# Layer 2's attention scores in the 64-row tile shape of the products, two heads per weight

## The chip, the cores and the metric

One Trainium2 chip, one of its cores. The metric is the device time of one launch in microseconds: the median of repeated runs. A profiled execution gives the trace; its span runs from the first to the last instruction on the core.

## The reference

Two rounds of attention and feed-forward over a sequence of 2048 tokens of width 448, all in bfloat16:

```python
x = x + A(layernorm(x)); x = x + B(layernorm(x))     # layers 0 and 1
x = x + A(layernorm(x)); x = x + B(layernorm(x))     # layers 2 and 3, same weights

def A(x):                       # H = 16 heads of 28
    q, k, v = heads(x @ wqkv)
    idx = pos[:, None] - 2 * arange(8)[None, :]      # 8 keys, every second token back
    logits = einsum("hsd,hswd->hsw", q, k[:, idx]) * 28**-0.5     # where idx >= 0
    return concat(einsum("hsw,hswd->hsd", softmax(logits), v[:, idx])) @ wo

def B(x):                       # width 1792, no nonlinearity
    return ((x @ w_gate) * (x @ w_up)) @ w_down
```

## The kernel before

The tokens are held with even and odd ones apart (two halves of 1024 columns), so that every second token back becomes the last eight columns of the same half. The sequence is cut into chunks of 256 or 512 tokens for each layer, and `SEQ` names the order of the chunk jobs: attention chunks (`A00` is layer 0, chunk 0) are mixed with feed-forward chunks, so that one layer's small matmuls lie among another's large products.

Nothing is scheduled at run time. Python code records operations (`sc.add`) with their engine, dependences and PSUM banks, and the tables `ORD` (for each engine, the order of operations by number) and `BANK` (the banks each takes) say in full how they stand. Waits are derived from the dependences. In `ORD["pe"]` an entry such as `253+349@24.30.42` means that a run of small matmuls (253) is cut at those places and strips of a large product (349, its host) are put in the gaps; a letter after `!` only orders waits.

The work of one attention chunk:

- `ln_chunk` normalises blocks of 128 tokens (VectorE, two small ScalarE steps), and `xn_sb` is transposed into `xnT`, by TensorE in the head of the kernel (`Tps`, line 638), else by DMAs on SyncE's queue.
- `qk_chunk` makes queries and keys (`WQK`): `twin` runs each product as two row halves of the array at once, 64 rows by 128 columns each; a unit's second half waits for its first half on TensorE itself (`crossed`). The result is copied to `qk` by ScalarE or VectorE (line 732). A head of 28 takes 32 rows, so four heads stand in 128 rows.
- `v_group` makes values, one product for two query blocks, copied to `v_sb` in one instruction (line 824). The last four heads' values go another way, through DRAM (`PW`, `VT`, on SyncE).
- `attn_front` makes scores of a group of two query blocks (120 queries each, 128 keys each, in two halves `c` of 64 keys): 64 matmuls of 28 rows by 64 columns (line 842), for each of 4 head columns, 2 blocks, 2 key halves and 4 heads; then two exponentials on ScalarE (line 849) and two mask multiplications on VectorE (line 859, `MK`). The first group has one block and 32 matmuls.
- `attn_back` multiplies with the values (line 879, 64 rows by 32 columns), `norm` divides, and `y_blocks` makes the output product with `wo_g`.

`b_chunk` makes gate and up (`Gps`, `Ups`), copies one (`G`, line 970), multiplies (`H`, line 973) and makes the down product (`WD`). Plain products are recorded in line 362, strips of hosts in lines 365 and 369. Warm-up matmuls (line 535) fill the head; weights are copied into `WQK` in line 544, mostly by GpSimd, which also makes the masks (lines 515, 519).

Of the kernel before, what the change touches and what calls it, by code (L numbers as in the profile page):

```python
# [3 lines left out]
dt = mybir.dt  # L4
ACT = mybir.ActivationFunctionType
ALU = mybir.AluOpType
# [49 lines left out]
FILL = 9  # L56
ORD = {
# [56 lines left out]

# [9 lines left out]
class Sched:  # L124
# [21 lines left out]
    def schedule(self):  # L146
# [29 lines left out]
        for e in self.ENGS:  # L176
            for x in ORD[e].split():
                ids, _, hint = x.partition("!")
                ids, _, cuts = ids.partition("@")
                ids, _, pre = ids.partition("~")  # L180
                burst, *hosts = [self.ops[int(i)] for i in ids.split("+")]
                pre = int(pre or 0)
                if pre:
                    for op in hosts:
                        take(op, e)
                    order[e].append((hosts, [(op, n) for op in hosts for n in range(2 * pre)], hint[:1]))
                    hint = hint[1:]
                    take(burst, e)
                else:
                    for op in (burst, *hosts):  # L190
                        take(op, e)
                seq = [(burst, n) for n in range(len(burst.ins))]
                if hosts:
                    strips = self.strips(x, hosts, pre, len(cuts.split(".")))
                    done = pre + len(strips) // len(hosts)
                    seq, a = [], 0
                    for i, z in enumerate([int(c) for c in cuts.split(".")] + [len(burst.ins)]):
                        seq += [(burst, n) for n in range(a, z)]
# [4 lines left out]
                order[e].append(([burst] if pre else [burst, *hosts], seq, hint))  # L203
# [194 lines left out]
def build(nc, A_x, A_wqkv, A_wo, B_w_gate, B_w_up, B_w_down, out):  # L398
# [35 lines left out]
    ones32 = sb([128, 128], bf, "ones32")  # L434
    MK = sb([128, 3, 72], bf, "MK")
    ident = sb([128, 128], bf, "ident")
# [679 lines left out]
```

## Time and profile before

| | |
|---|---|
| median of 3 runs | 384.57 us (384.23 to 384.86) |
| profiled execution | 384.47 us, span 382.7 us |
| TensorE | busy 377.9 us (99%), 6406 matmuls |
| VectorE | busy 268.9 us (70%) |
| ScalarE | busy 198.7 us (52%) |
| GpSimd | busy 10.4 us (3%) |
| granted TensorE clock | 0.999 of full speed |

Line numbers are those of the kernel before. A matmul's row gives its operand as rows * columns of the weight, then the moving operand. Matmuls overlap in the array, so the time of a stretch is read from the start of its first matmul to the start of the next stretch.

### The profile page before, as it was taken

How to read it: one execution, taken by the hardware profiler on the slowest of the kernel's cores; microseconds unless marked ns; L12 is line 12 of the kernel's file. 1: busy time of each engine (PE TensorE's matmuls, PEld its weight loads, DVE VectorE, ACT ScalarE, POOL GpSimd, SP SyncE). 2: the span in 40 equal slices, each digit the busy share in tenths (PEclk: the TensorE clock that was granted, in tenths of full speed). 3: DMA queues.
4: the chain of work that ended last, by engine and by line, in shares of the span. 5: the costliest groups of instructions: out<-in, count | busy, mean ns of one | idle time of the engine just before them, and what ended most of it. 6: DMA issues, size and time to landing. Idle time of an engine off the chain costs nothing.

```text
span 382.7 us, 14257 instructions
## 1 busy us (share of the span) xinstructions
PE 377.9 (99%) x6406; PEld 209.3 (55%) x6406; DVE 268.9 (70%) x595; ACT 198.7 (52%) x393; POOL 10.4 (3%) x42
## 2 busy tenths in 40 slices
PE   8999999999999999999999999999999999999997
PEld 3556477544555445445466677544555544445764
DVE  5986989788886584885868766666787786355413
ACT  4989986646635672345343664457435542124310
POOL 7210000000000000000000000000000000000000
PEclk9999999999999999999999999999999999999999
DMA  8967422500540026010411425120142005030003
GB/s 271 240 138 204 111 65 44 90 6 15 81 48 16 17 49 77 15 27 15 70 24 29 46 40 83 40 26 4 21 93 45 14 2 108 2 70 6 2 2 120
DMA packets 55103, 22.75 MB, mean 59 GB/s; under 512 B 46132, under 2 KB 54148, under 8 KB 55044
## 3 DMA queue, kind: packets, MB, share of 16 engines
q1 hardware_dynamic: 54612, 21.34, 27.8%
q8 instruction: 50, 0.82, 0.9%
q10 hardware_dynamic: 432, 0.52, 0.4%
q14 instruction: 9, 0.07, 0.1%
HBM read 8.54 MB, written 2.71 MB: 29 GB/s over the span
## 4 chain that ended last, share of the span: by engine, by line
PE 99%; ACT 0%; DVE 0%; issue 0%
PE ps L362 88%; PE ps L842 3%; PE ps L365 2%; PE ps L879 2%; PE ps L535 2%; PE ps L985 1%; PE ps L638 1%; ACT qk L732 0%; PE ps L369 0%; DVE x_sb L989 0%; DVE hT L499 0%; DVE eps_sb L499 0%
## 5 line engine op out<-in xcount | busy, mean ns | idle before, releaser
L362 PE MATMUL ps<-xnTb,WGU 64*128 64x512 bf16 (+1 forms) x1922 | 175.1, 333 | 0.0
L362 PEld LDWEIGHTS ps<-xnTb,WGU 64*128 64x128 bf16 x1922 | 92.6, 94 | 72.1 <-ACT g_sb L970 0.9
L970 ACT ACTIVATE g_sb<-ps 128x512 bf16<-128x512 f32 (+1 forms) x140 | 69.5, 510 | 99.6 <-PE ps L362 91.3
L973 DVE TENSOR_TENSOR hT<-g_sb,ps 128x512 bf16<-128x512 bf16 (+1 forms) x140 | 77.5, 575 | 43.5 <-ACT g_sb L970 42.3
L362 PE MATMUL ps<-WD,hT 64*128 64x448 bf16 x802 | 82.5, 349 | 0.0
L934 DVE TENSOR_TENSOR x_sb<-x_sb,ps 128x448 bf16<-128x448 bf16 x62 | 36.5, 615 | 40.0 <-PE ps L362 39.9
L362 PEld LDWEIGHTS ps<-WD,hT 64*128 64x128 bf16 x802 | 38.3, 94 | 33.9 <-DVE hT L973 0.2
L362 PE MATMUL ps<-xnTa,WQK 64*128 64x512 bf16 (+1 forms) x498 | 53.7, 352 | 0.2
L607 DVE BATCH_NORM_STATS2 st<-x_sb 128x6 f32<-128x448 bf16 x64 | 38.2, 612 | 1.8 <-DMA x_sb<-in_A_x_dram 1.6
L849 ACT ACTIVATE E_sb<-ps 128x1024 bf16<-128x1024 f32 (+1 forms) x36 | 34.1, 982 | 10.0 <-PE ps L842 9.5
L628 DVE TENSOR_SCALAR xn_sb<-x_sb,mv,rstd 128x512 bf16<-128x512 bf16 (+1 forms) x64 | 35.9, 569 | 3.5 <-ACT rstd L612 3.5
L362 PEld LDWEIGHTS ps<-xnTa,WQK 64*128 64x128 bf16 x498 | 22.9, 94 | 21.9 <-PE ps L362 1.2
L732 ACT ACTIVATE qk<-ps 128x1024 bf16<-128x1024 f32 (+1 forms) x28 | 25.7, 934 | 10.7 <-PE ps L362 10.1
L362 PE MATMUL ps<-wo_g,oT 64*128 64x448 bf16 x256 | 29.0, 349 | 0.1
L859 DVE TENSOR_TENSOR E_sb<-E_sb,MK 128x1024 bf16<-128x1024 bf16 (+2 forms) x40 | 23.6, 607 | 5.5 <-ACT E_sb L849 5.3
L905 ACT ACTIVATE R_sb<-R_sb 128x480 f32<-128x480 f32 (+1 forms) x34 | 20.2, 601 | 11.4 <-DVE R_sb L904 11.4
L917 DVE TENSOR_TENSOR oT<-O_sb,R_sb 128x480 bf16<-128x480 f32 (+3 forms) x36 | 21.9, 623 | 3.0 <-ACT R_sb L906 2.8
L904 DVE STREAM_SHUFFLE R_sb<-O_sb 128x480 f32<-128x480 f32 (+1 forms) x34 | 23.3, 693 | 0.0
L362 PE MATMUL ps<-WV,xnTa 64*128 64x336 bf16 (+3 forms) x252 | 23.2, 304 | 0.0
L610 ACT ACTIVATE lnv<-mv,eps_sb 128x2 f32<-128x2 f32 (+1 forms) x33 | 9.6, 295 | 22.6 <-DVE mv L609 22.5
L906 ACT ACTIVATE R_sb<-R_sb 128x480 f32<-128x480 f32 (+1 forms) x34 | 19.8, 599 | 0.1
L362 PEld LDWEIGHTS ps<-wo_g,oT 64*128 64x128 bf16 x256 | 12.2, 94 | 11.0 <-PE ps L362 0.5
(56 smaller groups left out, 193.7 us busy)
## 6 DMA issues: line engine op xcount, KB each, us to landing
out_dram<-x_sb SPq DMA_DIRECT2D x15, 112.0 KB, 1.8
WGU<-in_B_w_gate_dram SPq DMA_DIRECT2D x7, 224.0 KB, 4.2
WGU<-in_B_w_up_dram SPq DMA_DIRECT2D x7, 224.0 KB, 4.1
x_sb<-in_A_x_dram SPq DMA_DIRECT2D x3, 448.0 KB, 6.1
WD<-in_B_w_down_dram SPq DMA_DIRECT2D x2, 448.0 KB, 4.2
WD<-in_B_w_down_dram SPq DMA_DIRECT2D x2, 336.0 KB, 4.1
vt<-qk SPq DMA_DIRECT2D x42, 16.0 KB
xnTb<-xn_sb SPq DMA_TRANSPOSE x32, 3.0
```

The source lines that it names most:

```text
L362: return lambda E: E.matmul(out(), lhs(), rhs(), start=start, stop=stop)
L607: sc.add("dve", one(lambda E, B=B: E.bn_stats(st6[:, B, :], x_sb[:, B, :]), ("bn", li, B)), 525.0, deps=[("x", li - 1, B)] + ([("xn", li - ...
L628: sc.add("dve", one(lambda E, B=B, dst=dst, src=src: E.tensor_scalar(dst, src, mv[:, B, 0:1], rstd[:, B:B + 1], ALU.subtract, ALU.mult), ( ...
L732: return E.activation(dst, src, ACT.Copy) if hasattr(E, "activation") else E.tensor_copy(dst, src)
L849: return E.activation(E_sb[:, slot, 2 * hp:2 * hp + 2, 0:w], ps[:, b0:b0 + 2, 0:w], ACT.Exp, scale=SCALE)
L859: return E.tensor_tensor(e, e, m, ALU.mult)
L904: sc.add("dve", one(lambda E: E.stream_shuffle(R_sb[:, rs, 0:w], O_sb[:, os_, 0:w], [DH] * 32), ("Rs", li, qb)), dve_est(w) + 100.0, deps= ...
L905: sc.add("act", one(lambda E: E.activation(R_sb[:, rs, 0:w], R_sb[:, rs, 0:w], ACT.Ln), ("Rl", li, qb)), act_est(w, False), deps=[("Rs", l ...
L917: return E.tensor_tensor(oT[:, :, a % HALF:a % HALF + z - a], O[:, :, a - tok:z - tok], R_sb[:, rs, 0:w].rearrange("p (h n) -> p h n", h=4 ...
L934: sc.add("dve", one(lambda E: E.tensor_tensor(x_sb[:, B, :], x_sb[:, B, :], ps[:, bk[w], 0:D], ALU.add), ("x", li, B)), dve_est(D), deps=[ ...
L970: sc.add("act", one(lambda E, gs=gs, bk=bk: E.activation(g_sb[:, gs, 0:nt], ps[:, bk[0], 0:nt], ACT.Copy), ("G", li, j, fc)), act_est(nt), ...
L973: sc.add("dve", one(lambda E, gs=gs, bk=bk, fc=fc: E.tensor_tensor(hT[:, fc, hs, 0:nt], g_sb[:, gs, 0:nt], ps[:, bk[1], 0:nt], ALU.mult), ...
```

## The change

Layer 2's scores (`attn_front2`). For each half `c` of the keys, two operations copy the keys, each multiplied by a per-partition mask `pm` that keeps every second head, into `KB`: a block-diagonal weight, 64 rows by 128 columns, with the even head's 64 keys in one half of the columns and the odd head's in the other. 32 matmuls in place of 64 then give a group's scores, in two runs of 16, one for each `c`, each with its own two banks, exponential and mask multiplication. The copies go to GpSimd or VectorE.

What this brings with it: heads are laid out in another order (`head_at`, in `WQK` and `wo_g`); layer 2's keys take only half of `qk`'s columns (`key_col`), and `KB` takes the other half, in two slots, so later chunks wait for earlier readers (`old_readers`); even heads' values stand in the other half of the rows (three copies in `v_group` instead of one, and `lo` in `attn_back`); masks in that layout (`MB`) are put together by eight small DMAs. The single value group of layer 2 is cut 224 and 112 columns instead of 168 and 168.

`ORD` and `BANK` are new throughout, on all engines. Several short runs can now stand as one (`|`), some warm-up matmuls behind the first transposes are shorter (`FILLN`), and 12 of 18 stand ahead of them instead of 15. On GpSimd 28 of the 36 key copies come behind the weight copies of the head, which now come behind most of the mask operations.

```diff
+FILLN = {12: 128, 13: 64, 14: 64, 16: 64, 17: 64}
...
+def head_at(hc, b):
+    return 8 * (b % 2) + 2 * hc + b // 2
...
+        if li:
+            return attn_front2(li, g, prio, slot, prev)
...
+        KB = qk[:, 0, :, HALF + 512 * ks:HALF + 512 * ks + 512].rearrange("p h (d c n) -> p h d c n", d=2, c=2)
+        for c in range(2):
+            bk = Banks(2, pair=True)
...
+            war = [("S2", li, g - 2, c)] if g >= 2 else old_readers(HALF + 512 * ks, HALF + 512 * ks + 512)
+            for t in range(2):
+                lo = 64 * (c if t else 1 - c)
...
+                        return E.tensor_scalar(dst, src, pm[:, t:t + 1], None, ALU.mult)
...
+                sc.add(("pool", "dve"), ins, {"pool": 110.0 * len(ins) + 256 * nd * 1.04, "dve": 90.0 * len(ins) + 256 * nd * 0.55}, deps=[("QK", li, j, h) for a in k0 for j in chunks_of(li, a, a + 64) for h in range(4)] + war + PMD, prio=prio)
...
+            for hc, d, p in [(hc, d, p) for hc in range(4) for d in range(nd) for p in range(2)]:
+                qs, o = qb_info(qbs[d])[2] + 56 * c, (hc * nd + d) * nc
+                ins.append((lambda E, hc=hc, d=d, p=p, c=c, qs=qs, o=o, bk=bk: E.matmul(ps[:, bk[p], o:o + nc], KB[64 * p:64 * p + 64, hc, d, c, :], qk[64 * p:64 * p + 64, 1, hc, qs:qs + nc],
+                                                                                       start=True, stop=True), None))
...
+            sc.add("act", one(fe, ("Ex", li, g, c)), act_est(2 * w), deps=[("S2", li, g, c), prev], release=[(bk, 0), (bk, 1)], prio=prio)
...
+            sc.add(("act", "dve"), [(odd, None), (lambda E: even(E, 0), None), (lambda E: even(E, 64), [("V", li, q) for q in qbs])],
...
+            lo = 64 * (c if li == 0 or b % 2 else 1 - c)
+            vw = v_sb[lo:lo + 64, vslot[q], 32 * h:32 * h + 32] if t < 0 else v2_sb[lo:lo + 64, v2slot[q], 32 * t:32 * t + 32]
```

More of the change, by code (lines that the diff above doesn't have):

```diff
@@ L180, in schedule @@
                 ids, _, pre = ids.partition("~")
-                burst, *hosts = [self.ops[int(i)] for i in ids.split("+")]
+                bursts, *hosts = ids.split("+")
+                bursts, hosts = [self.ops[int(i)] for i in bursts.split("|")], [self.ops[int(i)] for i in hosts]
                 pre = int(pre or 0)
@@ L187, in schedule @@
                     hint = hint[1:]
[L188 to L192, printed above, removed]
+                for op in bursts if pre else bursts + hosts:
+                    take(op, e)
+                seq = [(op, n) for op in bursts for n in range(len(op.ins))]
                 if hosts:
@@ L195, in schedule @@
                     done = pre + len(strips) // len(hosts)
-                    seq, a = [], 0
-                    for i, z in enumerate([int(c) for c in cuts.split(".")] + [len(burst.ins)]):
-                        seq += [(burst, n) for n in range(a, z)]
+                    short, seq, a = seq, [], 0
+                    for i, z in enumerate([int(c) for c in cuts.split(".")] + [len(short)]):
+                        seq += short[a:z]
                         a = z
@@ L202, in schedule @@
                     seq += [(op, n) for op in hosts for n in range(2 * done, len(op.ins))]
-                order[e].append(([burst] if pre else [burst, *hosts], seq, hint))
+                order[e].append((bursts if pre else bursts + hosts, seq, hint))
         assert len(seen) == len(self.ops)
@@ L433, in build @@
     oT = sb([128, 4, HALF], bf, "oT")
-    ones32 = sb([128, 128], bf, "ones32")
+    cst = sb([128, 4 * 72], bf, "cst")
+    ones32, ident = cst[:, 0:128], cst[:, 128:256]
+    MB = cst[:].rearrange("p (k n) -> p k n", k=4)
+    pm = sb([128, 2], dt.float32, "pm")
     MK = sb([128, 3, 72], bf, "MK")
-    ident = sb([128, 128], bf, "ident")
     warm = hT[:, FC - 1, 1, 0:512]
@@ L446, in build @@
     sem_names += [f"d_t{li}_{j}" for li in range(4) for j in range(len(CH[li]))]
-    sem_names += [f"d_p{li}_{j}" for li in (0, 2) for j in range(len(CH[li]))] + [f"d_v{g}" for g in range(n_grp())] + ["d_one", "d_stv"]
+    sem_names += [f"d_p{li}_{j}" for li in (0, 2) for j in range(len(CH[li]))] + [f"d_v{g}" for g in range(n_grp())] + ["d_one", "d_stv", "d_mb"]
     vt_all = nc.dram_tensor("vt", (256, S), bf, kind="Internal").ap()
@@ L503, in build @@
     memset("dve", wo_g[:], 0.0, "c_wo", 1000)
-    sc.add("pool", one(lambda E: E.memset(ident[:], 1.0), "i_id"), 600, prio=-46)
-    sc.add("pool", one(lambda E: E.affine_select(ident[:], ident[:], [[-1, 128]], ALU.is_equal, 0.0, base=0, channel_multiplier=1), "c_id"), 300, deps=["i_id"], prio=-46)
+    sc.add("pool", one(lambda E: E.memset(ident, 1.0), "i_id"), 600, prio=-46)
+    sc.add("pool", one(lambda E: E.affine_select(ident, ident, [[-1, 128]], ALU.is_equal, 0.0, base=0, channel_multiplier=1), "c_id"), 300, deps=["i_id"], prio=-46)
     sc.add("pool", one(lambda E: E.memset(WQK[:].rearrange("p c w (h e) -> p (c w h) e", e=32)[:, :, DH:32], 0.0), "c_wqk0"), 700, prio=-45)
@@ L530, in build @@
     madd(2, 4, 3, "c_mk2", ["i_x2", "i_y1"])
-    memset("pool", ones32[:], 1.0, "c_ones", 100)
+    memset("pool", ones32, 1.0, "c_ones", 100)
+    memset("dve", pm[:], 0.0, "i_pm", 60)
+    for b in range(4):
+        sc.add("dve", one(lambda E, b=b: E.memset(pm[32 * b:32 * b + DH, b % 2:b % 2 + 1], 1.0), ("pm", b)), 60, deps=["i_pm"], prio=-38)
+    for n, (k, src, dst) in enumerate([(0, 0, 0), (1, 1, 1), (1, 0, 0), (1, 0, 1), (2, 0, 0), (2, 0, 1), (0, 1, 0), (0, 1, 1)]):
+        slot = (0, 0, 1, 1, 2, 2, 3, 3)[n]
+        plain_dma("sp", MB[64 * dst:64 * dst + 64, slot, :], MK[64 * src:64 * src + 64, k, :], ("mb", n), "d_mb", deps=[f"c_mk{k}", ("vones",)] + [("Tps", 0, B) for B in range(NBLK) if f"0{[a <= 128 * B < z for a, z in CH[0]].index(True)}" in PE_T], lat=2000.0)
+    MBD = [("mb", n) for n in range(8)]
+    PMD = [("pm", b) for b in range(4)]
     wb = Banks(1)
@@ L534, in build @@
     for n in range(WARM + FILL):
-        ins = [(lambda E: E.matmul(ps[:, wb[0], 0:512], warm[:, 0:128], warm[:, 0:512], start=True, stop=True), ("warm", n))]
-        sc.add("pe", ins, 428.0 if n < WARM else 216.0, deps=["c_warm"], mode="F",
+        m = FILLN.get(n, 512)
+        ins = [(lambda E, m=m: E.matmul(ps[:, wb[0], 0:m], warm[:, 0:128], warm[:, 0:m], start=True, stop=True), ("warm", n))]
+        sc.add("pe", ins, m / (1.2 if n < WARM else 2.4), deps=["c_warm"], mode="F",
                acquire=wb if n == 0 else None, release=[(wb, 0)] if n == WARM + FILL - 1 else [], prio=-1e6 if n < WARM else 1e6, after=fill)
@@ L541, in fn @@
             def fn(E, c=c, w=w):
-                src = stage[:, 2 * D * c:2 * D * (c + 1)].rearrange("p (w h e) -> p w h e", w=2, e=DH)[:, :, 8 * w:8 * w + 8, :]
-                dst = WQK[:, c, :, 256 * w:256 * w + 256].rearrange("p w (h e) -> p w h e", e=32)[:, :, :, 0:DH]
-                return E.activation(dst, src, ACT.Copy) if hasattr(E, "activation") else E.tensor_copy(dst, src)
+                src = stage[:, 2 * D * c:2 * D * (c + 1)].rearrange("p (w t z q e) -> p w t z q e", w=2, t=2, z=2, e=DH)[:, :, :, w]
+                dst = WQK[:, c, :, 256 * w:256 * w + 256].rearrange("p w (q t e) -> p w t q e", t=2, e=32)[:, :, :, :, 0:DH]
+                if not hasattr(E, "activation"):
+                    return E.tensor_copy(dst, src)
+                E.activation(dst[:, 0], src[:, 0], ACT.Copy)
+                return E.activation(dst[:, 1], src[:, 1], ACT.Copy)
             sc.add(("act", "dve", "pool") if POOL_WQK else ("act", "dve"), one(fn, ("wqk", c, w)), {"act": 470.0, "dve": 330.0, "pool": 600.0}, deps=[("stg", c), "c_wqk0"], prio=-28)
@@ L698, in twin_blocks, with key_col, old_readers @@
         crossed(parts, deps, prio, pe_cols(D), acquire, keys[0][0] + "ps")
+    def key_col(li, t):
+        return t % HALF if li else t
+    def old_readers(a, z):
+        res = [("S", 0, qb) for qb in range(NQB) if qb_info(qb)[0] < z and sum(qb_info(qb)[2:]) > a]
+        return res + [("PW", 0, i) for i in chunks_of(0, a, z) if (0, i) not in NOPW]
     def qk_chunk(li, j, prio):
@@ L705, in qk_chunk @@
         war = []
+        r0 = key_col(li, c0)
         if li >= 2:
-            for qb in range(NQB):
-                k0, nk, tok, nq = qb_info(qb)
-                if k0 < c1 and tok + nq > c0:
-                    war.append(("S", li - 2, qb))
-            war += [("PW", li - 2, i) for i in chunks_of(li - 2, c0, c1) if (li - 2, i) not in NOPW]
+            war += old_readers(c0, c1) + [x for x in old_readers(r0, r0 + n) if c0 >= HALF]
+            if c0 >= HALF:
+                war += [("KB", li, g, c, t) for g in range(n_grp()) if qb_info(grp_qbs(g)[0])[0] < c1 - HALF for c in range(2) for t in range(2)]
+                war += [("PW", li, i) for i in chunks_of(li, c0 - HALF, c1 - HALF)]
         def unit(c):
@@ L728, in mk @@
             def mk(eng, bk=bk, c=c):
-                dst = qk[:, :, c, c0:c1]
+                k = qk[:, 0, c, r0:r0 + n]
+                dst = bass.AP(tensor=k.tensor, offset=k.offset, ap=[list(k.ap[0]), [4 * S + c0 - r0, 2], [1, n]])
                 def fn(E):
@@ L736, in qk_chunk @@
         for B in range(c0 // 128, c1 // 128):
-            readersA.setdefault((li, B), []).extend([("Kps", li, j, 3), ("Qps", li, j, 3)])
+            readersA.setdefault((li, B), []).extend([(k, li, j, c) for k in ("Kps", "Qps") for c in range(4)])
         for b, w in [(b, w) for b in range(4) for w in range(2) if b + w < 4 and (li, j) not in NOPW]:
-            src = qk[32 * b + DH:32 * b + 32, w, :, c0:c1]
+            src = qk[32 * b + DH:32 * b + 32, w, :, c0:c1] if w else qk[32 * b + DH:32 * b + 32, w, :, r0:r0 + n]
             dst = vt_dram[li].rearrange("(t w b r) n -> r w b t n", w=2, b=4, r=4)[:, w, b, :, c0:c1]
@@ L772, in v_group @@
         nv = (D if plain else VD) // (2 if split else 1)
+        nc2 = (D if plain else VD) - 224
         def out(which):
-            return ps[:, bk[which], 0:nv]
+            return ps[:, bk[which], 0:(224, nc2)[which] if split else nv]
         def lhs(which, dc, lo, hi):
@@ L779, in rhs @@
         def rhs(which, dc, lo, hi):
-            return WV[lo:hi, dc, nv * which:nv * which + nv] if split else WV[lo:hi, dc, 0:nv]
+            return WV[lo:hi, dc, 224 * which:224 + nc2 * which] if split else WV[lo:hi, dc, 0:nv]
         keys = tuple(("Vps", li, qbs[0], w) for w in range(2)) if split else tuple(("Vps", li, q) for q in qbs)
@@ L816, in v_group, with cp, odd, even @@
             return
+        if li:
+            def cp(E, dst, src):
+                return E.activation(dst, src, ACT.Copy) if hasattr(E, "activation") else E.tensor_copy(dst, src)
+            def odd(E):
+                dst = v_sb[0:nk, s0:s0 + n, 256:384].rearrange("p s (q e) -> p s q e", e=32)[:, :, :, 0:DH]
+                src = ps[0:nk, bk[1]:bk[1] + 1, 0:112] if split else ps[0:nk, bk[0]:bk[0] + 2, 224:VD]
+                return cp(E, dst, src.rearrange("p s (q e) -> p s q e", e=DH))
+            def even(E, lo):
+                dst = v_sb[lo:lo + 64, s0:s0 + n, 0:256].rearrange("p s (q e) -> p s q e", e=32)[:, :, :, 0:DH]
+                return cp(E, dst, ps[64 - lo:128 - lo, bk[0]:bk[0] + n, 0:224].rearrange("p s (q e) -> p s q e", e=DH))
+            sc.add(("act", "dve"), [(odd, None), (lambda E: even(E, 0), None), (lambda E: even(E, 64), [("V", li, q) for q in qbs])],
+                   {"act": sum(act_est(n * x) for x in (112, 224, 224)) + 2 * 130.0, "dve": sum(dve_est(n * x) for x in (112, 224, 224))},
+                   deps=list(keys) + [p for _, p in slots] + ["c_v"], release=[(bk, 0), (bk, 1)], prio=prio)
+            for B in blocks:
+                readersA.setdefault((li, B), []).extend(keys)
+            return
         def fn(E):
@@ L974, in b_chunk @@
                        deps=[("G", li, j, fc), ("Ups", li, j, fc)] + war, release=[(bk, 1)], prio=prio)
-        xslot_users[hs] = [("Gps", li, j, FC - 1), ("Ups", li, j, FC - 1)]
+        xslot_users[hs] = [(k, li, j, fc) for k in ("Gps", "Ups") for fc in range(FC)]
         users = []
```

49 lines of the change are left out of this document (43 added, 6 removed), and 10 rows, old and new, of the table ORD.

## Prediction

> **What bounds the kernel now.** I read the page first (busy shares, chain), then TensorE's timeline, then the groups by form for the other engines.
>
> ```profile
> span 382.7 us, 14257 instructions
> PE 377.9 (99%) x6406; PEld 209.3 (55%) x6406; DVE 268.9 (70%) x595; ACT 198.7 (52%) x393; POOL 10.4 (3%) x42
> PE 99%; ACT 0%; DVE 0%; issue 0%
> PE ps L362 88%; PE ps L842 3%; PE ps L365 2%; PE ps L879 2%; PE ps L535 2%; PE ps L985 1%; PE ps L638 1%; ACT qk L732 0%; PE ps L369 0%; DVE x_sb L989 0%; DVE hT L499 0%; DVE eps_sb L499 0%
> ```
>
> The chain that ended last is TensorE at 99%, and no other engine has a per cent of it. A busy TensorE is not yet an efficient one, so the timeline says what a product costs. Its first column is a start; the difference of two starts is what a stretch really took, since the printed durations overlap.
>
> ```profile
> 175.57 1.67 PE L362 MATMUL ps<-xnTb,WGU 64*128 64x512 bf16 x14
> 177.08 0.59 PE L362 MATMUL ps<-WV,xnTa 64*128 64x336 bf16 x6
> ...
> 181.33 5.13 PE L362 MATMUL ps<-xnTb,WGU 64*128 64x512 bf16 x46
> 186.39 0.28 PE L879 MATMUL ps<-E_sb,v_sb 64*32 64x64 bf16 x24
> 186.49 0.40 PE L365 MATMUL ps<-xnTb,WGU 64*32 64x512 bf16 x8
> 186.71 0.24 PE L879 MATMUL ps<-E_sb,v_sb 64*32 64x64 bf16 x16
> 186.76 0.43 PE L365 MATMUL ps<-xnTb,WGU 64*32 64x512 bf16 x8
> 186.98 0.30 PE L879 MATMUL ps<-E_sb,v_sb 64*32 64x64 bf16 x24
> 187.21 3.84 PE L362 MATMUL ps<-xnTb,WGU 64*128 64x512 bf16 x34
> 190.89 1.49 PE L362 MATMUL ps<-WD,hT 64*128 64x448 bf16 x14
> 192.31 0.71 PE L842 MATMUL ps<-qk 28*64 28x64 bf16 x64
> 192.95 0.94 PE L362 MATMUL ps<-xnTb,WGU 64*128 64x256 bf16 x14
> 193.72 0.54 PE L362 MATMUL ps<-WD,hT 64*128 64x448 bf16 x4
> ```
>
> Fourteen 512-column products take 177.08 - 175.57 = 1.51 us, 108 ns each; no row shows TensorE waiting. So what TensorE streams is the time, and a saving elsewhere is worth nothing. Fourteen 448-column products should take 1.51 x 448/512 = 1.32 us, but those ahead of the scores take 192.31 - 190.89 = 1.42: a change of tile shape costs about 0.10 us. The scores of one group of two query blocks take 192.95 - 192.31 = 0.64. With the change of shape, a group costs 0.74.
>
> **The change, part by part.** (1) Layer 2's scores. A group's 64 matmuls of 28 rows by 64 columns become 32 of 64 by 128, of 64 columns, in two runs of 16. The nearest row in that shape is the head's transposes.
>
> ```profile
> 25.20 0.28 PE L638 MATMUL ps<-ident,xn_sb 64*128 64x64 bf16 x8
> 25.31 1.68 PE L362 MATMUL ps<-xnTa,WQK 64*128 64x512 bf16 x14
> 26.82 0.28 PE L638 MATMUL ps<-ident,xn_sb 64*128 64x64 bf16 x8
> ...
> 128.33 0.34 PE L842 MATMUL ps<-qk 28*64 28x72 bf16 x32
> 128.60 7.73 PE L362 MATMUL ps<-xnTb,WGU 64*128 64x512 bf16 x70
> ```
>
> Eight take 25.31 - 25.20 = 0.11 us, 14.5 ns each with the next digit, and the 14 products behind them take 1.51 as ever: no change of shape is paid. A group then costs 32 x 14.5 = 0.46, so it saves 0.28; eight groups 2.2. The first, single group saves 0.27 + 0.10 - 16 x 16 ns = 0.1. Together **-2.3 us**. It stands on the path, as TensorE does nothing else meanwhile. The bounds are 0, if the new runs cost what the old did, and 8 x 0.74 = 5.9, which nothing can exceed.
>
> The Trainium skill speaks against this (TensorEngine Tiling (Array Packing), Theoretical Speedup): a contraction of at most 32 allows four row tiles, so 28-row matmuls in eight tiles should run faster than in two. By it the old scores would take 8 rounds of 29 ns, 0.23 us, and the change would cost about 0.23 a group, +1.9 in all. The measured 0.64 decides against it; the same page (Key Properties) names the drain of a mode switch, with which the 0.10 agrees.
>
> (2) Products with values and their hosts. A lone run of 64 is this:
>
> ```profile
> 69.07 0.68 PE L879 MATMUL ps<-E_sb,v_sb 64*32 64x64 bf16 x64
> 69.68 0.60 PE L362 MATMUL ps<-WV,xnTa 64*128 64x336 bf16 x6
> ```
>
> That is 0.61, with the switch 0.71. With two cuts that hold strips of a product it is 187.21 - 186.39 = 0.82, less 16 strips (four whole products, 0.43): 0.39, with the switch 0.49. In layer 0 the new order puts two lone runs together (one switch, -0.10), gives two more a host (-0.22, and about -0.15 for the one with a single cut) and takes the host from one (+0.1). Layer 2 has as many hosted runs as before. **-0.4 us**, between 0 and -0.7. The single value group of layer 2 is cut 224 and 112 instead of 168 and 168: by columns 7 pairs at 224/512 of 0.216 instead of 168/512, **+0.15**.
>
> (3) The head.
>
> ```profile
> 8.40 2.94 PE L362 MATMUL ps<-xnTa,WQK 64*128 64x256 bf16 x42
> 11.29 0.29 PE L638 MATMUL ps<-ident,xn_sb 64*128 64x64 bf16 x8
> ...
> 23.26 0.70 PE L842 MATMUL ps<-qk 28*64 28x64 bf16 x64 [0.55 <-ACT qk L732]
> ...
> L515 POOL TENSOR_SCALAR_AFFINE_SELECT hT<-hT 128x72 bf16<-128x72 bf16 x16 | 3.6, 249 | 0.2
> L544 POOL COPY WQK<-hT 128x448 bf16<-128x448 bf16 x6 | 3.2, 558 | 2.0 <-DMA hT<-in_A_wqkv_dram 2.0
> ```
>
> Fewer warm-up matmuls free the first transposes some 0.6 us earlier, but it gains nothing: GpSimd now makes its masks ahead of the weight copies. From 2.8 us it has ten selects (2.2 us in 3.6/16 steps), two memsets, five copies or adds and one more select before the copy that the first product needs, which ends near 8.3; the first product starts at 8.40 today. Behind it, 42 products of 256 columns take 2.89 us, where 14 take 193.72 - 192.95 = 0.77 in the steady part: 0.58 too much, as a unit's second half waits for its first on TensorE itself. The new order puts another unit between them, which takes some 0.4 away, and moves eight transposes (0.12) into the wait of 0.55 at 23.26. VectorE's normalisations are then next late. **-0.45 us**, between -1.0 and +0.5.
>
> (4) New work off the path. Keys are copied twice, masked, into block-diagonal weights: 36 operations, 28 on GpSimd, 8 on VectorE, mostly of 512 elements. Value copies of layer 2 go from one instruction to three, on ScalarE or VectorE.
>
> ```profile
> L628 DVE TENSOR_SCALAR xn_sb<-x_sb,mv,rstd 128x512 bf16<-128x512 bf16 x32 | 12.7, 408 | 1.3 <-ACT rstd L612 1.3
> L732 ACT ACTIVATE qk<-ps 128x1024 bf16<-128x1024 f32 x22 | 22.2, 1024 | 10.1 <-PE ps L362 9.6
> sum 175.00, PE 175.00 PEld 96.58 DVE 124.31 ACT 88.63 POOL 0.00; mean PE 25.00 PEld 13.80 DVE 17.76 ACT 12.66 POOL 0.00
> 5.27 0.38 DVE L628 TENSOR_SCALAR xn_sb<-x_sb,mv,rstd 128x512 bf16<-128x512 bf16 x1
> 5.95 0.57 DVE L628 TENSOR_SCALAR xn_sb<-x_sb,mv,rstd 128x512 bf16<-128x512 bf16 x1 [0.30 <-ACT rstd L612]
> ```
>
> From 125 to 300 us VectorE is busy for 124 of 175 us and GpSimd for none, so throughput covers it: 8 x 0.41 = 3.3 us and some 6 us of value copies. The order is what matters. A key operation costs 0.41 on VectorE; on GpSimd no row has one. The copy's 558 ns for 448 elements gives 0.64; the ends I keep are 0.41 and, doubled, 1.3. Two places are tight:
>
> The third group: GpSimd does six operations, and TensorE's second run of 16 needs the last. From the last query-key product to that run TensorE has 28 value products (2.0), 16 output products (1.5), 28 gate-up products (3.0) and 16 scores (0.2): 6.8 us. The last two copies out of PSUM, 1.02 each on ScalarE, and the pipeline (0.25) take 2.3 of it. That leaves 4.5, or 0.74 an operation: 3.8 at 0.64, a margin of 0.6.
>
> The first group: 4.2 us from the last query-key product to its second run. The copy takes 1.3, VectorE four key operations, one addition (0.6) and a fifth, 2.4: a margin of 0.5.
>
> But both engines work at once there, and the two last rows show what that does: VectorE's 0.38 became 0.57 while a GpSimd copy ran. Five to eight such overlaps, 0.19 each, use up both margins: **+0.6 us**, between 0 and 1.9. Behind a late run, its exponential, its mask and the next gate-up product wait.
>
> Eight small mask DMAs go on SyncE's queue, five of them ahead of the transposes of layer 1's second chunk.
>
> ```profile
> 64.81 2.59 SPq L631 DMA_TRANSPOSE xnTb<-xn_sb  x2
> 68.15 2.67 SPq L631 DMA_TRANSPOSE xnTb<-xn_sb  x2
> ```
>
> A transpose takes that queue 1.3 us, a plain issue less than half; as the new order also puts one value transpose less ahead of these, the queue carries about 1 us more up to there, and 1 us is the price if nothing covers it. I take nothing: these four wait for data today, with a gap between the two rows. The order's end is covered too: VectorE's last gate product is ready about a microsecond behind its matmul, with 14 products (1.3) between.
>
> **Sum** against the profiled execution's own 384.47 us (span 382.7): -2.3 - 0.4 + 0.15 - 0.45 + 0.6 = -2.4, 382.1; that run stands 0.1 below the median of those shown, so **382.2 us**.
>
> **Rivals.** *Key operations too slow on GpSimd* (slower than before). From 0.74 us each the third group is late, from 0.9 the eighth also (five operations in 4.5 us). At 1.3 that is 6 x 1.3 - 4.5 = 3.3 and 5 x 1.3 - 4.5 = 2.0, and nearly 1 at the first: some 6 instead of 0.6, so 387.6. For it: no row has this operation with a per-partition operand. Against: copy and memset (528 ns for 512) agree. Above 1.05 us the gain is gone. Chance 0.13.
>
> *Each engine waits out the other's operation.* Then the first group loses 1.4 us of GpSimd operations against its 0.5, so 0.9, and the third 1.2 (two key operations and a normalisation of 0.41) against 0.6, so 0.6, with half a microsecond elsewhere: 2.0 instead of 0.6, 383.6. The Trainium skill has it so (SBUF — State Buffer, Terms: the shared port pair, on which the loser "fully blocks"). The row's 0.19 is less than the 0.4 that was left of that copy, so it speaks for half. Chance 0.15.
>
> *The new runs save nothing*: they cost 0.74, as a mixture of shapes or bank conflicts would make them; 384.5. The transposes speak against. Chance 0.05, and 0.03 more for the four-row-tile rule of part 1, 386.4.
>
> *A cold clock.* TensorE stands idle about 1 us more before the first query-key product; if the clock falls back to the 427 ns step of warm-up, some 3 us of products take twice as long: 383.7 or more. Chance 0.06.
>
> **How the numbers follow.** My own case keeps 0.58, at 381.2 to 383.2. A measurement here tells 0.2%, 0.8 us, from no change. Faster by more than that, below 383.8: my case, the blocked ports mostly, the clock mostly: 0.78. Within: 0.07. Slower: 0.13 and the tiling rule with a little of the ports: 0.15. The range 380.8 to 384.6 takes in the head's and hosts' ends below, the ports and the clock above, and leaves out the slow GpSimd.
>
> **What would show it.** Right: score runs of 16 in 0.23 us with no longer product ahead; key operations on GpSimd at 0.6 to 0.7; the first query-key product near 8.3; TensorE idle under a microsecond between 120 and 300. Wrong: key operations above 0.8, TensorE waiting ahead of layer 2's scores for GpSimd or VectorE, gate-up products waiting for banks, or a first product after 9.

## The result, and the profile after

The changed kernel takes 400.59 us (median of 4 runs, 400.32 to 400.96) where the kernel before takes 384.40: 1.0423 times as long, with a 95% interval from 1.0404 to 1.0442. The forecast was 382.2, in a range that ended at 384.6. It was wrong in sign; the rival that names slow key operations on GpSimd (387.6, chance 0.13) named the mechanism and gave a fifth of the loss. Of one experiment below (the late masks alone) the profiled execution took 649.63 us at a granted clock of 0.559, and it is not read.

The page of the changed kernel, its first lines and its chain of waits (line numbers from here on are those of the kernel that is shown, so they shift a little where an experiment adds lines):

```profile
span 398.3 us, 13731 instructions
PE 377.5 (95%) x6116; PEld 217.6 (55%) x6116; DVE 274.8 (69%) x612; ACT 204.9 (51%) x406; POOL 53.9 (14%) x73
PE 83%; POOL 12%; ACT 4%; DVE 1%; issue 0%; POOLq 0%
```

TensorE's share fell from 99% to 95%, and GpSimd, which had no per cent of the chain before, now has 12. Its groups by form say why; the last two numbers ahead of the idle time are the busy time and the mean of one in ns:

```profile
L939 POOL TENSOR_SCALAR qk<-qk,pm 128x512 bf16<-128x512 bf16 x25 | 39.7, 1605 | 222.3 <-ACT qk L761 221.5 <-PE ps L946 0.8
L939 POOL TENSOR_SCALAR qk<-qk,pm 128x256 bf16<-128x256 bf16 x4 | 3.7, 928 | 0.0
L561 POOL COPY WQK<-hT 128x448 bf16<-128x448 bf16 x6 | 3.2, 554 | 0.0
```

A key operation takes 1.6 us, not 0.64. TensorE's waits, in total, times and longest, show who pays:

```profile
PE ps L946 <- POOL qk L939: 11.5, 5, 4.3
PE ps L657 <- DVE xn_sb L647: 1.9, 1, 1.9
PE ps L946 <- DVE v_sb L849: 1.2, 1, 1.2
```

Line 946 is layer 2's scores. The third row's wait is GpSimd's too: in the timeline of the third group, below, the run at 182.31 stands 0.1 us behind 182.21, where the second key operation of the batch ends, and it needs that one; VectorE was done 0.8 us earlier.

```profile
178.95 9.83 POOL L939 TENSOR_SCALAR qk<-qk,pm 128x512 bf16<-128x512 bf16 x6 [47.63 <-ACT qk L761]
```

```profile
182.31 0.41 PE L946 MATMUL ps<-qk 64*128 64x64 bf16 x16 [1.20 <-DVE v_sb L849]
...
188.83 0.61 PE L946 MATMUL ps<-qk 64*128 64x64 bf16 x16 [3.85 <-POOL qk L939]
189.25 5.86 PE L367 MATMUL ps<-xnTb,WGU 64*128 64x512 bf16 x42
195.04 0.28 PE L980 MATMUL ps<-E_sb,v_sb 64*32 64x64 bf16 x24
```

Six operations from 178.95 end at 188.78, and the group's second run starts at 188.83. Behind the wait 42 products take 195.04 - 189.25 = 5.79 us instead of 4.53: the clock has fallen. A table by stretches (length, busy time, instructions, granted clock, DMA share, GB/s) shows it:

```profile
183.30:188.80 5.50, 1.69 (x16) 0.95 0.16 24
188.80:195.00 6.20, 6.17 (x58) 0.77 0.19 37
195.00:200.00 5.00, 5.00 (x148) 1.00 0.02 3
```

What the change was for is there as well. Two runs of 16 in a row:

```profile
198.46 1.49 PE L367 MATMUL ps<-WD,hT 64*128 64x448 bf16 x14
199.78 0.63 PE L946 MATMUL ps<-qk 64*128 64x64 bf16 x32
200.25 0.93 PE L367 MATMUL ps<-xnTb,WGU 64*128 64x256 bf16 x14
```

The group takes 0.47, and the 14 products ahead of it 1.32, no 0.10 more: a group at 0.47 instead of 0.74.

To see where time went, I added up in each trace the steady times of all products in their order (108 ns for one of 512 columns, 94.6 for 448, and so on, 345 us in all) and took from each the time at which equal sums are reached. The difference against the kernel before, in us, minus meaning ahead:

| products done, us | what has passed | changed | keys in order of need | all four rearrangements |
|---|---|---|---|---|
| 0 | first product | +1.18 | -0.58 | -0.90 |
| 12 | head | +0.25 | -1.41 | -1.68 |
| 102 | layer 0 | +0.67 | -0.74 | -1.62 |
| 150 | groups 1, 2 | +1.12 | -1.11 | -1.99 |
| 180 | groups 3, 4 | +7.33 | -1.22 | -2.10 |
| 234 | groups 5, 6 | +9.21 | -1.46 | -2.39 |
| 276 | groups 7 to 9 | +15.64 | -2.48 | -3.40 |

The two last columns are experiments. Most of the loss is made at three places in layer 2: the third group, the sixth, and the seventh and eighth.

### The profile page after: what moved, and what is told of

It reads as the page before. It is cut to its first block, busy times and chain, and to the rows that moved or that the text cites. A ratio compares the mean times of both kernels' runs of the same rounds, so it can differ in the third digit from the quotient of the medians.

```text
span 398.3 us, 13731 instructions
## 1 busy us (share of the span) xinstructions
PE 377.5 (95%) x6116; PEld 217.6 (55%) x6116; DVE 274.8 (69%) x612; ACT 204.9 (51%) x406; POOL 53.9 (14%) x73
## 4 chain that ended last, share of the span: by engine, by line
PE 83%; POOL 12%; ACT 4%; DVE 1%; issue 0%; POOLq 0%
PE ps L367 75%; POOL qk L939 9%; ACT qk L761 3%; PE ps L370 2%; PE ps L980 2%; PE ps L890 1%; PE ps L1086 1%; PE ps L946 1%; POOL hT L522 1%; POOL WQK L561 1%; ACT E_sb L897 1%; POOLq L1166 0%; DVE E_sb L907 0%; PE ps L657 0%; ACT v_sb L870 0%
## 5 line engine op out<-in xcount | busy, mean ns | idle before, releaser
L367 PE MATMUL ps<-xnTb,WGU 64*128 64x512 bf16 (+1 forms) x1922 | 178.7, 336 | 0.0
L367 PEld LDWEIGHTS ps<-xnTb,WGU 64*128 64x128 bf16 x1922 | 96.1, 95 | 69.4 <-issue 3.6
L367 PE MATMUL ps<-WD,hT 64*128 64x448 bf16 x812 | 84.0, 349 | 0.0
L939 POOL TENSOR_SCALAR qk<-qk,pm 128x512 bf16<-128x512 bf16 (+1 forms) x29 | 43.3, 1512 | 222.3 <-ACT qk L761 221.5
L367 PEld LDWEIGHTS ps<-WD,hT 64*128 64x128 bf16 x812 | 40.6, 94 | 31.8
L647 DVE TENSOR_SCALAR xn_sb<-x_sb,mv,rstd 128x512 bf16<-128x512 bf16 (+1 forms) x64 | 37.6, 607 | 0.5 <-ACT rstd L631 0.3
L367 PEld LDWEIGHTS ps<-xnTa,WQK 64*128 64x128 bf16 x498 | 25.0, 94 | 20.8 <-ACT E_sb L897 0.7
L761 ACT ACTIVATE qk<-ps 128x1024 bf16<-128x1024 f32 (+1 forms) x30 | 27.8, 949 | 8.8 <-PE ps L367 8.8
L952 ACT ACTIVATE E_sb<-ps 128x1024 bf16<-128x1024 f32 (+1 forms) x18 | 17.7, 981 | 16.4 <-PE ps L946 16.2
L946 PE MATMUL ps<-qk 64*128 64x64 bf16 (+1 forms) x272 | 7.3, 196 | 12.8 <-POOL qk L939 11.5
```

The source lines that it names most:

```text
L367: return lambda E: E.matmul(out(), lhs(), rhs(), start=start, stop=stop)
L647: sc.add("dve", one(lambda E, B=B, dst=dst, src=src: E.tensor_scalar(dst, src, mv[:, B, 0:1], rstd[:, B:B + 1], ALU.subtract, ALU.mult), ( ...
L761: return E.activation(dst, src, ACT.Copy) if hasattr(E, "activation") else E.tensor_copy(dst, src)
L939: return E.tensor_scalar(dst, src, pm[:, t:t + 1], None, ALU.mult)
```

## Experiments

Theory A: not GpSimd's speed alone, but the order of its queue, which puts operations that are needed first behind others. Rival B: 28 operations of 1.6 us are too much in any order. The 28 stand in the table `ORD`, three for groups 1 and 2, then a batch for each chunk.

**Order of need.** Only the numbers of the key copies in GpSimd's list are moved (the third group's second run needs 937 and 936, the first 942):

```diff
-787 774 770 936 942 967 963 968 937 1155 1181 1156 1160 ...
+774 770 787 942 936 937 963 967 968 1155 1156 1160 1181 ...
```

> The 28 key copies of GpSimd stand in its queue in the order in which TensorE's score runs need them; nothing else is changed, each still takes 1.56 us. In the changed kernel a score run of the third group waits for the sixth copy of its batch, of which it needs only the third, one of the eighth group for the last of ten. Theory A, the queue's order: copies at 1.56 us are quick enough if the needed ones come first. Third copy 3 x 1.56 = 4.7 us behind 178.9, at 183.6, where the run could stand at about 182.5: TensorE waits at most 2 us in all between 120 and 300 us instead of about 17, and the time is 384 to 387. Theory B, the speed alone: 28 copies of 1.56 us are too much for the stretches that hide them in any order; at least 6 us of waits stay, time above 390.

Measured: 382.08 us, the median of ten runs from 381.49 to 389.32 (ratio to before 0.9956, interval 0.9927 to 0.9984). The operations are as slow as ever, and TensorE hardly waits. From this kernel's groups and its timeline of GpSimd and TensorE:

```profile
L939 POOL TENSOR_SCALAR qk<-qk,pm 128x512 bf16<-128x512 bf16 x25 | 39.5, 1596 | 74.0 <-ACT qk L761 74.0
```

```profile
176.72 12.88 POOL L939 TENSOR_SCALAR qk<-qk,pm 128x512 bf16<-128x512 bf16 x8 [46.69 <-ACT qk L761]
```

```profile
181.62 0.41 PE L946 MATMUL ps<-qk 64*128 64x64 bf16 x16 [0.23 <-POOL qk L939]
181.86 4.70 PE L367 MATMUL ps<-xnTb,WGU 64*128 64x512 bf16 x42
186.49 0.28 PE L980 MATMUL ps<-E_sb,v_sb 64*32 64x64 bf16 x24
```

One wait of 0.23 is left of 12.7, and the 42 products take 186.49 - 181.86 = 4.63. Theory A holds and B falls. The time is below the 384 to 387 that A expected, and 1.66 us of that is the head, whose order is the same and which was quicker in this execution (-1.41 against +0.25 in the table).

**One operation moved.** The changed kernel with 937 third in its batch instead of sixth.

```diff
-936 942 967 963 968 937
+936 942 937 967 963 968
```

> The changed kernel with one operation moved: in GpSimd's queue the key copy for the third group's second score run stands third in its batch instead of sixth. Theory A, the order: its wait of 3.85 us goes, and with it the slow clock behind it (42 products in 5.79 us instead of 4.53), together about 5 us; the waits of the sixth and the eighth group stay: 394.5 to 396.5. If the speed alone decides: the other copies of the batch come late instead, and less than 2 us go.

```profile
183.85 0.41 PE L946 MATMUL ps<-qk 64*128 64x64 bf16 x16 [1.20 <-DVE v_sb L849]
...
186.37 0.41 PE L946 MATMUL ps<-qk 64*128 64x64 bf16 x16
186.60 4.71 PE L367 MATMUL ps<-xnTb,WGU 64*128 64x512 bf16 x42
191.24 0.28 PE L980 MATMUL ps<-E_sb,v_sb 64*32 64x64 bf16 x24
```

The wait of 3.85 is gone and the clock stays up (191.24 - 186.60 = 4.64). At equal work the stretch of the third and fourth groups costs 0.9 us instead of 6.2. The time was 396.96 (one run), above the 394.5 to 396.5 expected; this execution has another wait, in the head, of 2.0 us (below).

**What the operation costs, by form.** Three kernels, order as in the changed one, with another operation on GpSimd alone. The first two leave the mask out, so scores of two heads are mixed:

```diff
-return E.tensor_scalar(dst, src, pm[:, t:t + 1], None, ALU.mult)
+return E.tensor_copy(dst, src)                                   # plain copy
+return E.tensor_scalar(dst, src, 1.0, None, ALU.mult)            # number
+return E.tensor_tensor(dst, src, m.to_broadcast(...), ALU.mult)  # two tensors, m a bf16 mask column
```

> GpSimd's key copies leave the mask out and are plain copies (so the other head's keys stand in the weight and the scores are mixed); order and everything else as in the changed kernel. Theory A, the form of the operation: a plain copy takes 0.55 us for 448 elements in the head, so 0.6 to 0.65 here, the waits of 17 us ahead of layer 2's scores go, and the time is 383 to 385, which then shows what the rest of the change is worth. Theory B, the access (strided source and destination in one tile): copies take over 1.2 us too, and the time stays above 390. Theory C, the port shared with VectorE: durations scatter with VectorE's work between 0.6 and 1.5.

> GpSimd's key copies multiply by the number 1 instead of the mask column (mask left out, scores mixed). If the per-partition operand is what costs, they take 0.6 to 0.7 us and the time is 383 to 385; if the multiplication is, they stay at 1.56 us and the time at 400.

> GpSimd's key copies multiply two tensors, keys and a bf16 mask column read with a step of zero, so the result is the masked copy again. The additions of 72 elements on GpSimd take 0.32 us where a copy of 64 takes 0.25. If only the per-partition operand of the other form is slow: 0.7 to 1.1 us an operation and 383 to 387 us. If any multiplication is slow there: 1.4 us or more, and 395 to 402.

Their groups in this order, a fence for each:

```profile
L940 POOL COPY qk<-qk 128x512 bf16<-128x512 bf16 x25 | 15.2, 648 | 232.4 <-ACT qk L761 226.3 <-PE ps L948 6.1
```

```profile
L940 POOL TENSOR_SCALAR qk<-qk 128x512 bf16<-128x512 bf16 x25 | 38.0, 1543 | 224.3 <-ACT qk L761 223.8 <-PE ps L948 0.6
```

```profile
L948 POOL TENSOR_TENSOR qk<-qk,pmb 128x512 bf16<-128x512 bf16 x25 | 25.8, 1060 | 227.7 <-ACT qk L766 225.9 <-PE ps L956 1.9
```

A copy with the same strides takes 0.65, a product of two tensors 1.06, a product with a number 1.54, with a column 1.60. So it is neither the access nor the operand kept per partition: the scalar form itself is slow there. Times: 382.49 us (median of ten runs from 381.78 to 388.86; 0.9965, interval 0.9943 to 0.9988), 399.71 and 387.54 (one run each). With quick copies the first order costs nothing, 382.49 against 382.08 for the slow operation in the order of need. The loss needed both, the slow operation and this order: to change either one removes it.

**The head.** In the changed kernel's profile the second normalisation and GpSimd's copies stand so:

```profile
5.82 0.38 POOL L522 TENSOR_SCALAR_AFFINE_SELECT hT<-hT 128x72 bf16<-128x72 bf16 x1
6.14 2.06 POOL L561 COPY WQK<-hT 128x448 bf16<-128x448 bf16 x4
```

```profile
6.12 2.23 DVE L647 TENSOR_SCALAR xn_sb<-x_sb,mv,rstd 128x512 bf16<-128x512 bf16 x1
```

```profile
9.57 2.80 PE L367 MATMUL ps<-xnTa,WQK 64*128 64x256 bf16 x48 [0.38 <-POOL MK L526]
```

0.38 us of work took 2.23 and ended 0.15 behind the four copies; the first product came at 9.57. With the same order in the head, the kernel with keys in order of need shows 0.81 and a first product at 7.82. In that profile, the three with another form and the one with one operation moved, this normalisation took 0.41 to 0.81 and had started 0.03 to 0.15 us ahead of the first of the four copies; here it started 0.02 ahead. So a few hundredths of a microsecond went with 1.4 us or more. Two kernels on top of the order of need make the one case or the other certain; GpSimd's list, weight copies in brackets:

```diff
-... [75] 30 40 [79 76 77 78] 41 [82] 36 42        # changed kernel
+... [75 76 79 82 77 78] 30 40 41 36 42            # solid
+... [75 76] 28 [79] 31 [82] 29 [77] 35 [78] 32 ...  # selects between
```

> Key copies in the order of need, and in the head GpSimd's six weight copies stand in one block, with the mask operations that lay between them behind it (in the changed kernel one copy, two mask operations, four copies, one mask operation, one copy). VectorE normalises the first two blocks of tokens under this block. Theory L, the lock: an operation of VectorE that asks for the port while GpSimd's copies follow each other waits until the last of them has ended, as in the changed kernel's profile, where a normalisation took 2.23 us from 6.12 to 8.35 beside four copies. Then the two normalisations end near 8.3 or later in every run, the first query-key product stands at 9.3 to 9.8, and the time is 1 to 2 us above that of the order of need alone (383 to 384.5). Rival H, half speed: both go on at once and the normalisation takes at most 0.8 us, as it does in the profile of the order of need alone (0.81); the copies end 0.5 us earlier, the first product stands at 7.5 to 8 and the time is 381.5 to 382.3.

> Key copies in the order of need, and in the head a mask operation between nearly all weight copies of GpSimd, which start as their data land (4.1 us) ahead of the remaining masks. Theory L: VectorE gets the port in the gaps, both normalisations take at most 0.9 us, the first product stands at 7.4 to 7.9 and the time is 381.3 to 382. Rival: the lock is taken again before VectorE gets it, a normalisation takes over 1.5 us and the first product comes at 9 or later, 383 or more.

Solid block, GpSimd, VectorE, TensorE:

```profile
5.03 3.07 POOL L561 COPY WQK<-hT 128x448 bf16<-128x448 bf16 x6
```

```profile
5.56 3.34 DVE L647 TENSOR_SCALAR xn_sb<-x_sb,mv,rstd 128x512 bf16<-128x512 bf16 x2
```

```profile
9.85 1.46 PE L367 MATMUL ps<-xnTa,WQK 64*128 64x256 bf16 x12
```

Selects between:

```profile
5.34 1.10 DVE L647 TENSOR_SCALAR xn_sb<-x_sb,mv,rstd 128x512 bf16<-128x512 bf16 x2
```

```profile
7.79 2.79 PE L367 MATMUL ps<-xnTa,WQK 64*128 64x256 bf16 x48 [0.51 <-ACT WQK L563]
```

Two normalisations take 3.34 us under the block, ending at 8.90 behind the last copy (8.10), and 1.10 between selects; the times are 385.51 (1.0034, interval 1.0023 to 1.0045) and 381.76 (0.993, 0.9912 to 0.9947). Theory L holds for these copies. That agrees with the Trainium skill (SBUF — State Buffer, Terms: the port pair that VectorE and GpSimd share is exclusive, and the loser waits out the whole instruction); here the wait went on over the copies that followed.

Beside GpSimd's key operations the rule as cited does not come out. In the changed kernel a key copy of VectorE took 0.78 us, the one ahead of it 0.35, but it ended 0.7 us before the operation of GpSimd that had started ahead of it; there the measurement decides:

```profile
178.95 1.72 POOL L939 TENSOR_SCALAR qk<-qk,pm 128x512 bf16<-128x512 bf16 x1 [47.63 <-ACT qk L761]
```

```profile
179.16 0.78 DVE L939 TENSOR_SCALAR qk<-qk,pm 128x512 bf16<-128x512 bf16 x1
```

The 3.75 us between the two kernels are more than the wait. The first product stands 2.06 later (9.85 against 7.79). Behind TensorE's wait of 2.23 in the solid kernel 48 products then took 4.21 us, 2.68 in the changed kernel, at a granted clock of 0.61; the 383 to 384.5 expected did not count that:

```profile
9.80:14.10 4.30, 4.25 (x51) 0.61 0.84 245
```

**The head alone.** The changed kernel with only the selects between, keys in their first order.

> The changed kernel with only the head's part mended: selects between GpSimd's weight copies, the key copies in their first order. At equal work the changed kernel's profile is 0.25 us behind the kernel before at the end of the head, the order of need with selects between is 0.6 to 1.2 ahead. Theory: head and key copies add up. Then 398.6 to 399.8, 0.8 to 2 below the changed kernel, and the waits ahead of layer 2's scores stay at 11 to 13 us. Rival: what the head gains is given back at the first of these waits, as the key copies come when they come; 400.3 to 401.

Measured: 400.21 (1.0444, interval 1.037 to 1.0517), in four runs at 398.2, 398.5, 401.9 and 403.4. Its profile is one of 398.5, has the 11.5 us of waits for key copies unchanged, and is 1.8 ahead at the end of the head. So head and keys add up in that execution, as expected, and something else took 3.4 to 5 us from two runs. The median lies between the two expectations and does not decide.

**The second DMA transpose.** In the profiles of the number and of the one moved operation TensorE waits in the head for the transpose of layer 0's last tokens. From the one with the number:

```profile
30.48 0.50 PE L367 MATMUL ps<-xnTa,WQK 64*128 64x256 bf16 x6 [2.03 <-DMA xnTa<-xn_sb]
30.80 1.64 PE L367 MATMUL ps<-WV,xnTa 64*128 64x448 bf16 x8
32.20 3.50 PE L367 MATMUL ps<-xnTa,WQK 64*128 64x256 bf16 x42
```

Eight products behind it take 1.40 instead of 0.76. Two rearrangements of SyncE's list, the transposes (209, 211) side by side and the mask DMAs (49 to 56) late, were tried apart and together; the last row is the masks alone, without selects between:

```diff
-209 98 211 100 ...                                   # selects between
+209 211 98 100 ...                                   # + transposes side by side
-312 310 527 110 54 520 ... 50 ... 51 ... 55 ... 53 ... 52 ... 49 56
+... 738 740 49 50 51 52 53 54 55 56                  # + masks late = all four
```

> Key copies in the order of need, selects between the head's weight copies, and on SyncE's queue the two DMA transposes of layer 0's last two blocks of tokens stand next to each other, ahead of a weight load that lay between them. In two profiles with a quick head (plain numbers, one operation moved) TensorE waited 2.0 us at 28.5 us for the second of them, and the clock fell behind that: some 4 us in all. Theory D: this wait, which comes and goes with the landing of DMAs, is why single runs of the order of need alone stand at 383.9 to 389 beside 381.5 to 382.3. Then no run stands above 383 any more, and the median is 381.2 to 381.9. If the scatter has another source, single runs above 383.5 stay.

> As the kernel with the paired transposes, with the eight mask DMAs behind layer 2's first transposes as well. The value transposes of layer 0 are then no longer behind four of them, and the wait of 0.5 to 0.7 us at 61 us should go: 380.6 to 381.3, 0.4 to 0.8 below the kernel without it. If the value transposes are late for another reason, no difference over 0.2 us.

> Key copies in the order of need, and the eight mask DMAs of SyncE's queue stand together behind the transposes of layer 2's first chunk (113 us) instead of between 48 and 103 us. In the order of need alone TensorE waits 0.70 us at 61 us for a transpose of values on that queue, behind four of these DMAs. If they cost what the queue lacks: that wait goes and 0.6 to 0.9 us with it, 381.2 to 381.6. If the value transposes wait for something else (their data, the other small DMAs): the wait stays, no difference over 0.3 us.

| kernel | median | runs | ratio to before, interval |
|---|---|---|---|
| transposes side by side | 382.03 | 381.74 to 382.35 (4) | 0.9943, 0.9927 to 0.9959 |
| all four | 381.25 | 381.12 to 381.66 (5) | 0.9923, 0.991 to 0.9935 |
| masks late alone | 382.99 | the rest 381.50 to 385.56 (9) | 0.9969, 0.9943 to 0.9995 |

The median of the late masks alone counts the run of 649.63; at 382.99 it missed the 381.2 to 381.6 expected.

With the transposes side by side no run stands apart any more (9 here and 10 in the next kernel). Without, single runs stood 2 to 7 us above the others in four kernels (order of need, plain copies, late masks, head alone), though in none of the four runs with selects between alone and of the nine with the solid block. That agrees with this wait as a source. It is likely rather than shown: the wait was seen in two kernels that ran once, and no profile of a high run beside low ones of the same kernel exists. It is not the only source either, as one run of the kernel before, which has the two transposes side by side, took 387.24, 3 us above its 14 neighbours. The median did not gain: 382.03 against 381.76 with selects between alone, where 381.2 to 381.9 was expected.

The masks explain less than expected, though 381.25 for all four lies within the 380.6 to 381.3 expected. TensorE's wait for the value transposes, without and with the late masks:

```profile
60.85 0.68 PE L980 MATMUL ps<-E_sb,v_sb 64*32 64x64 bf16 x64 [0.38 <-DMA v_sb<-vt]
```

```profile
60.37 0.68 PE L980 MATMUL ps<-E_sb,v_sb 64*32 64x64 bf16 x64 [0.16 <-DMA v_sb<-vt]
```

It shrinks by 0.2 and does not go, where the medians are 0.8 apart. Of the rest, 0.3 us stand between the two profiles before the first mask DMA is issued at 49.01: the same output products start at 48.87 without and at 48.57 with the late masks. So the traces give the masks 0.2; what makes the remainder is open.

**What the scores save.** All four rearrangements, each score run of layer 2 issued twice.

```diff
+            ins = ins + ins
             ins[-1] = (ins[-1][0], ("S2", li, g, c))
```

> The kernel of all four rearrangements with each of layer 2's 18 score runs issued twice (the second set writes the same scores again). If a run costs what the prediction said, 16 x 14.5 ns with no change of shape, this adds 16 runs x 0.232 + 2 x 16 x 16.2 ns = 4.2 us less what falls into waits: 3.8 to 4.4 us. If a hidden cost of the shape or of PSUM comes with each run (0.10 us), it adds 5.8 to 6.2 us.

385.42 against 381.25: 4.17 us for 18 runs, 4.2 expected. That prices the matmuls. A doubled run has no more changes of shape than a single one, so it can't show what a change costs; that none is paid is read from the rows above (1.32 for the 14 products ahead of a group, 0.47 for the group).

All four rearrangements together are the best version: 3 us below the kernel before, 19 below the changed one, with the same instructions in another order.

## Why the prediction was wrong

**Term 4, the key operations, is the step that failed.** It read the price of an operation on GpSimd from a copy (558 ns for 448 elements) and carried it to a multiplication. For a copy that was right, 0.65 with the same access. For the operation that is there it was wrong by 2.5 times, and the end of the range that was kept, 1.3, did not reach it. A copy, a select and a memset, which agreed, all lacked the multiplication; agreement among them was no evidence for it.

**The rival had the place and two thirds of the waits.** At the measured 1.56, its own formula gives 6 x 1.56 - 4.5 = 4.9 at the third group (1.20 + 3.85 = 5.05 measured) and 5 x 1.56 - 4.5 = 3.3 at the eighth, where the queue made a run wait for the last of its batch (5.4 in two waits, ahead of the seventh and of the eighth). It missed the sixth group (1.69), and the clock: behind the waits of 3.85 and 4.30 products and runs took about 3 us too much. The prediction had a cold clock for the head only, as a rival of its own. The Trainium skill's rule (TensorE: Matmul & The Clock Gate, Part 1: The HAM clock gate: half clock behind an idle window of some 3.4 us) fits these, not the waits of 2.03 and 2.23 in the head, behind which the granted clock was 0.58 and 0.61.

**It took the order as given.** It worked out for each group whether the batch of operations fits, not which run needs which of them. At the measured price the batches fit in the order of need, and do not in the order that is there. The kernel's own cost for the operation, 110 + 512 x 1.04 = 642 ns, is the same wrong price; that the order was made from it is likely, and was not tried.

**Term 1, scores: right.** 0.47 a group against the forecast 0.46, and 4.17 us for a second set. The changed rows show no change of shape paid, as it said. At equal work the stretch of layer 2 (102 to 276 in the table) saves 1.74 in the order of need; the forecast for it was -2.3 + 0.15 + 0.6 = -1.55.

**Term 2, hosts in layer 0: wrong.** Forecast -0.4. Between the head and layer 2 the best version gains nothing (-1.68 to -1.62) and the order of need loses 0.67, most of it a wait of 0.70 for value transposes. Which of the hosts gave what and which wait took it back was not taken apart further.

**Term 3, the head: wrong in size, both ways.** Forecast -0.45 between -1.0 and +0.5; -1.1 to -1.8 in the profiles where VectorE gets the port, +0.25 in the changed kernel's. It let the first product wait for a copy that ends near 8.3; in the order of need that product stood at 7.82, while the copy ended at 8.24. The rival of blocked ports priced this for layer 2 and not for the head, where plain copies follow each other.

**SyncE's mask DMAs** were taken at nothing with a price of 1 us ahead of layer 1's transposes. What was late was a transpose of values, and the mask DMAs made 0.2 us of that.

That the order of need ends at 382.08, next to the forecast of 382.2, is no merit: a better head and a worse layer 0 cancel.

## What to carry to other kernels

Take the price of an operation from a row with the same arithmetic, engine and operands, and where there is none, let the range reach well beyond the nearest row. When work moves to a slow engine that stands idle, compare its queue's order with the order in which the consumer needs the results; one operation three places too late cost over 5 us here. Count a wait of TensorE twice, once for itself and once for the clock behind it, and leave gaps between GpSimd's copies where VectorE must run beside them.

## What was not expected of the hardware

- GpSimd's multiplication by a number or a column took 1.5 to 1.6 us for 512 bf16 elements, longer than the product of two tensors (1.06); a copy took 0.65.
- It hardly depends on VectorE. From the group of the changed kernel's key operations (minimum, median and maximum in ns, over both sizes):

```profile
L939 POOL TENSOR_SCALAR qk<-qk,pm x29: 919/1563/1938, 127.8 to 288.0; 128x512 bf16<-128x512 bf16 x25, 128x256 bf16<-128x256 bf16 x4
```

  The median is 1.56, and operations with VectorE idle beside them took 1.56 as well.
- Four copies in a row kept a normalisation of 0.38 us from its end for 2.23 us; with a start some hundredths of a microsecond earlier it took 0.41 to 0.81 beside the same copies.
- A wait of 2.03 us in the head was followed by products at half speed (granted clock 0.58), and so was one of 2.23 (0.61). Behind waits of 1.69 in layer 2 and of 1.87 in the changed kernel's head the clock stayed at 1.00.
